# Scores of A's second head by VectorE as well, and the three units of a set in turn

## The chip, the cores and the metric

The kernel runs on one core of a Trainium2 chip. A core has TensorE (PE, matmuls; PEld are its weight loads), VectorE (DVE), ScalarE (ACT), GpSimd (POOL) and SyncE (SP, which here issues the loads); data comes from HBM into SBUF by DMA. The metric is the device time of one execution in microseconds: 1005.88 us, the median of three runs (1005.79 to 1005.91).

## The reference

One token is decoded by two attention blocks over the same input x (448 wide), and a gate mixes their outputs. Block A has 16 heads with a K and a V of their own, block B has 16 query heads on 8 K/V heads. Both caches hold 8192 keys of 256 floats.

```python
    def _A_ref(x, k_cache, v_cache, wq, wo):
        B, Sq, D = x.shape
        H, Dh = 16, 256
        q = (lambda x, *d: x.transpose(*d))((x @ wq).reshape(B, Sq, H, Dh), 0, 2, 1, 3)
        scores = jnp.einsum("bhqd,bhkd->bhqk", q, k_cache) * (Dh ** -0.5)
        p = _softmax(scores, axis=-1)
        o = jnp.einsum("bhqk,bhkd->bhqd", p, v_cache)
        return (lambda x, *d: x.transpose(*d))(o, 0, 2, 1, 3).reshape(B, Sq, H * Dh) @ wo
...
    x = A_x
    g = _sigmoid((x * gate_w).sum(-1, keepdims=True))
    a = _A_ref(x, A_k_cache, A_v_cache, A_wq, A_wo)
    b = _B_ref(x, B_k_cache, B_v_cache, B_wq, B_wo)
    return g * a + (1 - g) * b
```

`_B_ref` does the same with each K and V used for two query heads. All of it is float32. K and V of both blocks are 24 heads x 2 x 8.4 MB, 403 MB, and each byte is used once.

## The kernel before, in words

**Tiles and sets.** The heads are worked off in 8 sets. A set has three units: unit 2 is one K/V head of B with its two queries, units 0 and 1 are two heads of A. A unit's 8192 keys are cut into NT = 4 tiles of 16 rows on each of 128 partitions: a K tile and a V tile have 128 x 4096 floats, 2.1 MB each. TILES (line 35) is the order of all 96 tiles: set by set, in a set unit 2, then 0, then 1, and in a unit its four tiles.

**The stream.** The host lays everything that is read, K, V, wq and wo, into one array in the order of `plan()`. There the K tile with index i is followed by the V tile with index i - LEAD (LEAD = 3), so a V tile comes three tiles behind its K tile. The pieces are cut into loads of FULL = 15872 floats a partition (7936 KB), which go into a ring of SLOTS = 3 slots. SyncE issues a load when all work on the slot's former content is done, and the work on a load waits for the whole of it. The last loads are small: the last half load of V and K, the last V tile in pieces of 8, 4 and 4 rows, and the wo of the last set.

**Scores in two ways.** B's unit 2 and A's unit 1 are scored on TensorE (`scores`): the host has turned their K so that the head's dimension lies on partitions; 8 matmuls write the scores of a tile into PSUM (ps_sc), VectorE takes the minimum (mn), ScalarE the exponential (px), VectorE transposes it into pr. A's unit 0 is scored on VectorE (`scores_by_row`, the units in BY_ROW, line 32): K lies by rows, VectorE multiplies the tile in its slot with the head's query, which `spread` has copied to all partitions (qa), and sums each row (sr); then follow the minimum in three short operations, the exponential on ScalarE (pxr) and the spread into pr.

**The rest of a unit.** `attend` multiplies pr with the V tile on TensorE and adds up in PSUM (ps_o, three buffers, one for each unit under way). After a unit's last K tile, `gather`, `combine` and `column` bring the sums of its 128 partitions together (gs, mnr, ew, es, z, rz, wr, then sel); after its last V tile, `take` moves ps_o into ob by ScalarE and VectorE, and `project_o` makes from ob and sel the column ocs, which wo is multiplied with (`emit_set`, at the end `emit` and `emit_half`, into ps_y).

**What sets the order.** No scheduler: `build` walks through the loads, and `piece` writes the work of each piece in that order on all engines. `combine`, `column` and `project_o` are put off by one or two K tiles (`wait`, `tick`; among the last V tiles each V tile ticks). Each engine runs its instructions in the order written, and `Recorder` adds the semaphores.

Of the kernel before, what the change touches and what calls it, by code (L numbers as in the profile page):

```python
# [3 lines left out]
F32 = mybir.dt.float32  # L4
# [5 lines left out]
P = 128  # L10
D = 448
DH = 256
# [4 lines left out]
NG = 4  # L17
YN = D // NG

NS = 8  # L20
ROWS = 16
NT = NCOL // ROWS
FULL = 15872
LEAD = 3
BLK = 32
NB = ROWS
# [2 lines left out]
SLOTS = 3  # L29
WQ = (4 * KF + 2) * DH  # L30
UNITS = [2, 0, 1]
BY_ROW = {(s, 0) for s in range(NS)}
LAST_CUT = [8, 4, 4]
HEAD_AT = {2: 0, 0: 2, 1: 3}
TILES = [((s, r), t) for s in range(NS) for r in UNITS for t in range(NT)]


DEAL = {0: 8, 1: 7, 2: 8, 4: 8, 7: 8, 8: 8, 15: 8}
# [16 lines left out]
def plan():  # L55

    size = {"xg": XG, "k": ROWS * DH, "v": ROWS * DH, "wq": WQ, "wo": 8 * D}
    per = len(UNITS) * NT
    n = len(TILES)
    items = []  # L60
# [197 lines left out]
def build(nc, stream, dealt, out):  # L258
# [4 lines left out]
    small = Pool(nc, "small", 2)  # L263
# [6 lines left out]
    def heads(u):  # L270
        return 2 if u[1] == 2 else 1
# [6 lines left out]
    for M in (2, 1):  # L278
        r = R[M]
# [7 lines left out]
        CAP[M] = const.tile([P, NT], F32, name=f"cap{M}")  # L287
        nc.vector.tensor_scalar(CAP[M], mask, 3.0e38, OFF, op0=OP.mult, op1=OP.add)

    even = small.tile([P, NB * BLK], F32, name="px")[:, :P].rearrange("p (k n) -> p k n", k=2)  # L290
    nc.gpsimd.iota(even, pattern=[[1, 2], [2, P // 2]], base=0, channel_multiplier=-1,
                   allow_small_or_imprecise_dtypes=True)
    nc.vector.tensor_scalar(even, even, 0.0, None, op0=OP.is_equal)
    half = const.tile([P, 2], F32, name="half")
    nc.vector.tensor_reduce(half, even, axis=AX.X, op=OP.add)

    head2 = small.tile([P, NB * BLK], F32, name="px")[:, :P].rearrange("p (m n k) -> p m n k", m=2, k=2)
    nc.gpsimd.iota(head2, pattern=[[2, 2], [4, P // 4], [1, 2]], base=0, channel_multiplier=-1,
                   allow_small_or_imprecise_dtypes=True)
    nc.vector.tensor_scalar(head2, head2, 0.0, None, op0=OP.is_equal)  # L300
# [10 lines left out]

    in4 = const.tile([P, 2, NG], F32, name="in4")
    nc.vector.tensor_copy(in4[:, 0, :], rows4)
    block = small.tile([P, NB * BLK], F32, name="px")[:, :P].rearrange("p (g n) -> p g n", g=NG)
    nc.gpsimd.iota(block, pattern=[[BLK, NG], [1, BLK]], base=0, channel_multiplier=-1,
                   allow_small_or_imprecise_dtypes=True)
    nc.vector.tensor_scalar(block, block, 0.0, None, op0=OP.is_equal)
# [8 lines left out]
    for par in range(2):  # L326
        for r in (r for r in range(3) if (par, r) not in BY_ROW or (par + 2, r) not in BY_ROW):
            QB[par, r] = const.tile([P, 2, 64], F32, name=f"qb{par}{r}")
# [13 lines left out]
    def clear(t, n):  # L342
        nc.tensor.matmul(t[:, :n], zero, zero[:, None, :n // 4].to_broadcast([P, 4, n // 4]), start=True, stop=False, skip_group_check=True)
# [24 lines left out]
    ST, PR, O, GS, WR, SEL, OB, OC = ({} for _ in range(8))  # L368

    QR, SC, QA = {}, {}, {}  # L370

    def project(s, c0, w):

        if s not in QR:
            QR[s] = ps_s.tile([2 * BLK, 2 * DH], F32, name="sm")
        q = QR[s]
        if s == DS and c0 == KF:
            for j in range(DN):
                k = DN - 1 - j
                n = BLK if j == 0 else 1  # L380
                nc.tensor.matmul(q[:n, :], dx[:, k:k + n], dq[:, k, :], start=(j == 0), stop=False, skip_group_check=True)
        for j in range(w.shape[1]):
            a, c = divmod(c0 + j, KF)
            for a in (a,) if a < 2 else (0, 1):
                c = c if c0 + j < 2 * KF else KF
                nc.tensor.matmul(q[BLK * a:BLK * (a + 1), :], xz[:, c if c < KF else KF + a, :], w[:, j, :],
                                 start=(c == 0), stop=(c == KF), skip_group_check=True)
        if c0 + w.shape[1] == 2 * KF + 1:
            QR[s] = small.tile([P, NB * BLK], F32, name="px")[:2 * BLK, :2 * DH]
            nc.scalar.activation(QR[s], q, AF.Copy)  # L390

    def spread(s):

        qt = ps_s.tile([P, 2, 2, 2], F32, name="sm")
        qr = QR.pop(s)
        for h in range(2):
            for e in range(2):
                at = h * DH + e * P
                nc.tensor.matmul(qt[:, h, e, :], qr[:, at:at + P], rows4[:2 * BLK, :2], start=True, stop=True)
        for r, a, h, M in ((2, 0, 0, 2), (0, 1, 0, 1), (1, 1, 1, 1)):  # L400
            if (s, r) in BY_ROW:
                qa = ps_s.tile([P, DH], F32, name="sm")
                nc.tensor.matmul(qa, rows4[:2 * BLK, 1:2].to_broadcast([2 * BLK, P]), qr[:, h * DH:(h + 1) * DH], start=True, stop=True)
                QA[s, r] = small.tile([P, DH], F32, name="qa", bufs=1)
                nc.scalar.activation(QA[s, r], qa, AF.Copy, scale=-scale)
                continue
            nc.vector.tensor_scalar(QB[s % 2, r][:, :, BLK:BLK + M], qt[:, h:h + M, :, a].rearrange("p h e -> p e h"),
                                    -scale, None, op0=OP.mult)

    def scores(u, t, j0, kt):  # L410
        M = heads(u)
        if t == 0 and j0 == 0:
            ST[u] = small.tile([P, 2, NT], F32, name="st", bufs=4)
        if j0 == 0:
            SC[u, t] = ps_sc.tile([P, NB * BLK], F32, name="sc")
        sc = SC[u, t]
        qb = QB[u[0] % 2, u[1]]
        for j in range(kt.shape[1]):
            e, g = divmod(j0 + j, NG)
            at = BLK - R[M] * g - t * M  # L420
            nc.tensor.matmul(sc[32 * g:32 * (g + 1), :], qb[:, e, at:at + 32], kt[:, j, :],
                             start=(e == 0), stop=(e == 1), skip_group_check=True)
        if j0 + kt.shape[1] < 2 * NG:
            return
        st = ST[u]
        mn = small.tile([P, 1], F32, name="mn")
        nc.vector.tensor_reduce(mn, sc, axis=AX.X, op=OP.min)
        nc.vector.tensor_tensor(st[:, 0, t:t + 1], mn, CAP[M][:, t:t + 1], op=OP.min)
        px = small.tile([P, NB * BLK], F32, name="px")
        nc.scalar.activation(px, sc, AF.Exp, bias=st[:, 0, t:t + 1], scale=-1.0, accum_out=st[:, 1, t:t + 1])  # L430
        pr = small.tile([P, NB * BLK], F32, name="pr", bufs=LEAD + 1)

        nc.vector.transpose(pr.rearrange("p (q r k) -> p q k r", r=BLK, k=2),
                            px.rearrange("p (q k c) -> p q k c", c=BLK, k=2))
        PR[u, t] = pr.rearrange("p (q c) -> p q c", c=2 * BLK)
# [41 lines left out]
    def take(u):  # L477

        o = O.pop(u)
        ob1 = small.tile([P, NB * BLK], F32, name="px")[:, :DH]  # L480
        OB[u] = small.tile([P, DH], F32, name="ob")
        nc.scalar.activation(ob1, o[:, DH:], AF.Copy, scale=half[:, 1:2])
        nc.vector.scalar_tensor_tensor(OB[u], o[:, :DH], half[:, 0:1], ob1, op0=OP.mult, op1=OP.add)

    def gather(u):
# [3 lines left out]
        st = ST[u][:, :, None, :].to_broadcast([P, 2, NG, NT])  # L489
        if u in BY_ROW:  # L490
            nc.vector.tensor_tensor(GS[u][:, :, :, :, 0], st, in4[:, :, :, None].to_broadcast([P, 2, NG, NT]), op=OP.mult)
# [31 lines left out]
    def column(u):  # L523
        M = heads(u)
        cl = ps_s.tile([P, 1], F32, name="sm")
        nc.tensor.matmul(cl, WR.pop(u).rearrange("p c x m k -> p (c x m k)"), ones[:1, :], start=True, stop=True)
        SEL[u] = small.tile([P, 2], F32, name="sel")
        if M == 2:
            nc.vector.tensor_scalar(SEL[u], which, cl, None, op0=OP.mult)
        else:  # L530
            nc.scalar.activation(SEL[u][:, :1], cl, AF.Copy)
# [16 lines left out]

    def fold():

        yf = small.tile([P, NB * BLK], F32, name="px")
        nc.scalar.activation(yf[:, :D], YY[0], AF.Copy)
        YY[0] = ps_y.tile([P, D], F32, name="Y")
        clear(YY[0], YN)
        for g in range(NG):
            nc.tensor.matmul(YY[0][32 * g:32 * g + 1, :YN], any4, yf[:, g * YN:(g + 1) * YN], start=False, stop=False,
                             skip_group_check=True)
# [34 lines left out]
    def wait(n, f, *args):  # L592
        todo.append([n, f, args])

    def tick():
        for t in todo:
            t[0] -= 1
        for t in [t for t in todo if t[0] <= 0]:
            todo.remove(t)
            t[1](*t[2])  # L600

    def piece(kind, i, at, view):
        n = view.shape[-1] // ATOM[kind]
        j0 = at // ATOM[kind]
        if kind == "xg":
            inputs(view)
            GW[0] = view[:, KF + 1:DX]
        elif kind == "wq":
            project(i, j0, view.rearrange("p (c n) -> p c n", c=n))
            if j0 + n < 2 * KF + 1:  # L610
                pass
# [5 lines left out]
        elif kind == "k":  # L617
            u, t = TILES[i]
            if u in BY_ROW:
                scores_by_row(u, t, 2 * j0, view.rearrange("p (j d) -> p j d", d=DH))  # L620
# [9 lines left out]
        elif kind == "v":  # L630
            u, t = TILES[i]
            n = view.shape[-1] // DH
            attend(u, t, at // DH, n, view.rearrange("p (j d) -> p j d", d=DH))
            if at // DH + n == ROWS:
                if t == NT - 1:
                    take(u)
                    if u != TILES[-1][0]:
                        wait(1, project_o, u)
                if i >= len(TILES) - LEAD:
                    tick()  # L640
# [14 lines left out]
    for fill in LOADS:  # L655
        buf = ring.tile([P, FULL], F32, name="slot")
        c = 0
        for load in fill:
            n = sum(x[3] for x in load)
# [84 lines left out]
```

## Time and profile before

| what | before |
| --- | --- |
| median of three runs | 1005.88 us |
| the profiled execution's own time | 1005.68 us |
| its span, first to last instruction | 1004.0 us |
| mean granted TensorE clock | 0.765 |
| read from HBM | 433.07 MB |

The page cuts the span into 40 slices; a digit is a slice's busy share in tenths. These are the rows of TensorE, VectorE, the clock and the loads.

```profile
PE   1665754665653674656645565764665647645567
DVE  3287222962249521486115851248521585215851
PEclk9776687677776886787777867776887877877888
DMA  9999999999999999999999999999999999999998
```

VectorE's row goes up and down eight times, once a set: it is high while unit 0 is scored and low while TensorE scores the other two. The row of the DMA is the same throughout.

Most instructions are recorded under one source line, 198, where the kernel's helper issues them; the groups are told apart by the tiles that they write and read. In a row of a group stand the instruction, what it writes and reads, the shape, the count, then the busy time, the mean of one in ns, and the idle time ahead of it with what ended it. In a row of the timeline stand the start and the duration in us, and in square brackets an idle time ahead of it.

### The profile page before, as it was taken

The numbers are of one execution on the slowest core, as the hardware profiler recorded it, in microseconds if no ns is written. First come the engines' busy times: TensorE is split into PE (matmuls) and PEld (weight loads), VectorE is DVE, ScalarE is ACT, GpSimd is POOL, SyncE is SP. The second block draws the span as 40 slices with busy tenths as digits, with TensorE's granted clock in tenths as the row PEclk, the third lists the DMA queues.
The fourth block names the chain that finished last, engine by engine and source line by source line (L and its number), as shares of the span: only waits on it lengthen the run. The fifth ranks groups of instructions, "written<-read, shape, count | busy, mean of one in ns | idle before, by whom it ended". The sixth has DMA issues, their size and how long they took to land.

```text
span 1004.0 us, 7427 instructions
## 1 busy us (share of the span) xinstructions
PE 593.3 (59%) x3162; PEld 172.6 (17%) x3162; DVE 461.2 (46%) x645; ACT 94.2 (9%) x308; POOL 6.1 (1%) x12
## 2 busy tenths in 40 slices
PE   1665754665653674656645565764665647645567
PEld 0111211121111221112111121111211112111112
DVE  3287222962249521486115851248521585215851
ACT  0100110001100110001100010100110000110011
POOL 2000000000000000000000000000000000000000
PEclk9776687677776886787777867776887877877888
DMA  9999999999999999999999999999999999999998
GB/s 395 442 440 435 423 433 444 433 423 438 443 426 425 441 441 430 423 443 439 426 433 436 438 428 440 430 429 437 436 436 427 431 443 433 426 433 443 435 413 364
DMA packets 9544, 432.49 MB, mean 431 GB/s; under 512 B 1137, under 2 KB 1521, under 8 KB 2161
## 3 DMA queue, kind: packets, MB, share of 16 engines
q1 hardware_dynamic: 9364, 431.24, 99.3%
q0 software_dynamic: 144, 0.79, 0.2%
q8 instruction: 24, 0.39, 0.1%
q14 instruction: 8, 0.07, 0.0%
q10 hardware_dynamic: 4, 0.00, 0.0%
HBM read 433.07 MB, written 0.00 MB: 431 GB/s over the span
## 4 chain that ended last, share of the span: by engine, by line
DMA 71%; PE 15%; DVE 13%; ACT 1%; issue 1%; SPq 0%; DVEq 0%
DMA slot<-in_stream_dram 71%; PE ps_o L198 6%; PE ps_sc L198 6%; DVE sr L198 5%; DVE slot L198 5%; PE ps_s L198 2%; DVE pr L198 1%; ACT px L198 1%; DVE mn L198 1%; ACT ew L198 0%; DVE st L198 0%; DVE wr L198 0%; ACT pxr L198 0%; PE ps_y L198 0%; DVE mt L198 0%
## 5 line engine op out<-in xcount | busy, mean ns | idle before, releaser
L198 PE MATMUL ps_o<-slot,pr 128*32 128x512 f32 (+1 forms) x1536 | 350.7, 762 | 217.4 <-DMA slot<-in_stream_dram 217.3
L198 PE MATMUL ps_sc<-slot,qb 128*32 128x512 f32 x1024 | 201.7, 751 | 98.5 <-DMA slot<-in_stream_dram 98.4
L198 DVE TENSOR_REDUCE mn<-ps_sc 128x1 f32<-128x512 f32 x64 | 44.1, 690 | 327.5 <-PE ps_sc L198 301.9
L198 DVE TENSOR_TENSOR slot<-slot,qa 128x4096 f32<-128x4096 f32 (+7 forms) x40 | 142.6, 3564 | 36.4 <-DMA slot<-in_stream_dram 36.4
L198 PEld LDWEIGHTS ps_o<-slot,pr 128*32 128x32 f32 (+1 forms) x1536 | 80.4, 143 | 399.7 <-DMA slot<-in_stream_dram 245.4
L198 DVE TENSOR_REDUCE sr<-slot 128x16 f32<-128x4096 f32 (+7 forms) x40 | 142.7, 3566 | 1.4
L198 PEld LDWEIGHTS ps_sc<-slot,qb 128*32 128x32 f32 x1024 | 46.9, 134 | 220.5 <-issue 115.8
L198 ACT ACTIVATE px<-ps_sc,st 128x512 f32<-128x512 f32 x64 | 44.0, 687 | 401.9 <-DVE st L198 401.9
L198 DVE STREAM_TRANSPOSE pr<-px 128x512 f32<-128x512 f32 x64 | 45.7, 714 | 54.1 <-ACT px L198 54.1
L198 PE MATMUL ps_s<-slot,xz 128*32 128x512 f32 (+1 forms) x130 | 42.4, 652 | 28.3 <-DVE xz L198 22.1
L198 ACT ACTIVATE pxr<-sr,st 128x16 f32<-128x16 f32 x32 | 9.8, 307 | 365.1 <-DVE st L198 365.1
L198 PE MATMUL ps_s<-sel,ob 128*128 128x1 f32 (+1 forms) x96 | 18.1, 292 | 34.6 <-DVE ob L198 34.6
L198 DVE SCALAR_TENSOR_TENSOR ob<-ps_o,half,px 128x256 f32<-128x256 f32 x24 | 11.3, 472 | 58.5 <-ACT px L198 58.5
L198 PEld LDWEIGHTS ps_s<-sel,ob 128*128 128x128 f32 x96 | 16.0, 235 | 58.9 <-DVE ob L198 47.8
L198 DVE TENSOR_TENSOR pr<-pxr,cols 128x256 f32<-128x256 f32 x32 | 13.6, 426 | 16.9 <-ACT pxr L198 15.5
L198 PE MATMUL ps_y<-slot,ocs 128*1 128x448 f32 (+1 forms) x176 | 18.2, 500 | 3.8 <-DMA slot<-in_stream_dram 3.6
L198 PEld LDWEIGHTS ps_s<-slot,xz 128*32 128x32 f32 (+1 forms) x130 | 10.4, 122 | 54.4 <-issue 25.2
L198 ACT ACTIVATE px<-ps_o,half 128x256 f32<-128x256 f32 x24 | 11.3, 470 | 56.9 <-PE ps_o L198 56.7
L198 PE MATMUL ps_s<-ones,wr 1*128 1x1 f32 x48 | 10.0, 276 | 10.9 <-DVE wr L198 10.9
L198 PE MATMUL ps_s<-px,rows 64*128 64x256 f32 x16 | 7.0, 523 | 13.8 <-DVE es L198 13.8
L198 PEld LDWEIGHTS ps_s<-ones,wr 1*128 1x128 f32 x48 | 8.0, 207 | 34.6 <-DVE wr L198 17.0
L198 ACT ACTIVATION_READ_ACCUMULATOR px<-ps_sc,st 128x1 f32 x64 | 12.3, 193 | 0.0
(68 smaller groups left out, 152.3 us busy)
## 6 DMA issues: line engine op xcount, KB each, us to landing
slot<-in_stream_dram SPq DMA_DIRECT2D x48, 7936.0 KB, 41.2
slot<-in_stream_dram SPq DMA_DIRECT2D x1, 7904.0 KB, 48.5
slot<-in_stream_dram SPq DMA_DIRECT2D x1, 7712.0 KB, 43.8
slot<-in_stream_dram SPq DMA_DIRECT2D x1, 7688.0 KB, 21.0
slot<-in_stream_dram SPq DMA_DIRECT2D x1, 5120.0 KB, 42.3
slot<-in_stream_dram SPq DMA_DIRECT2D x2, 2048.0 KB, 32.7
slot<-in_stream_dram SPq DMA_DIRECT2D x1, 2816.0 KB, 35.8
slot<-in_stream_dram SPq DMA_DIRECT2D x2, 1024.0 KB, 31.2
```

What stands on the lines that cost most here:

```text
L198: i = getattr(e, what)(*args, **kw)
```

## The change

Unit 1 joins BY_ROW, so both A heads of each set are scored by VectorE from rows of K, and its K is laid out by rows in the stream. In TILES the loops over units and tiles change places, so a set's units alternate: tile 0 of unit 2, 0, 1, then tile 1 of the three, and so on. The buffers follow: px has one instead of two, qa four instead of one, sel four instead of two.

```diff
-BY_ROW = {(s, 0) for s in range(NS)}
+BY_ROW = {(s, r) for s in range(NS) for r in (0, 1)}
...
-TILES = [((s, r), t) for s in range(NS) for r in UNITS for t in range(NT)]
+TILES = [((s, r), t) for s in range(NS) for t in range(NT) for r in UNITS]
...
             if (s, r) in BY_ROW:
                 qa = ps_s.tile([P, DH], F32, name="sm")
                 nc.tensor.matmul(qa, rows4[:2 * BLK, 1:2].to_broadcast([2 * BLK, P]), qr[:, h * DH:(h + 1) * DH], start=True, stop=True)
-                QA[s, r] = small.tile([P, DH], F32, name="qa", bufs=1)
+                QA[s, r] = small.tile([P, DH], F32, name="qa", bufs=4)
...
-        px = small.tile([P, NB * BLK], F32, name="px")
+        px = small.tile([P, NB * BLK], F32, name="px", bufs=1)
...
-        SEL[u] = small.tile([P, 2], F32, name="sel")
+        SEL[u] = small.tile([P, 2], F32, name="sel", bufs=4)
...
-        return [t for s in range(NS) for r in UNITS
-                for t in (b[s] if r == 2 else by_row[2 * s + r] if by_row is not None and (s, r) in BY_ROW else a[2 * s + r])]
+        pick = lambda s, r: b[s] if r == 2 else by_row[2 * s + r] if by_row is not None and (s, r) in BY_ROW else a[2 * s + r]
+        return [pick(*u)[t] for u, t in TILES]
```

The other places that take a px tile get `bufs=1` in the same way.

How the instructions move is seen in the order in which they stand on each engine. At the end of the program VectorE had these rows before, from the minimum of the last set's next to last K tile (unit 1) to the end; the units' tiles share one name.

```order
L198 TENSOR_REDUCE mn<-ps_sc 128x1
L198 TENSOR_TENSOR st<-mn,cap_0 128x1
L198 STREAM_TRANSPOSE pr<-px 128x8x2x32
L198 SCALAR_TENSOR_TENSOR ob<-ps_o,half,px 128x256
L198 TENSOR_REDUCE mn<-ps_sc 128x1
L198 TENSOR_TENSOR st<-mn,cap_0 128x1
L198 STREAM_TRANSPOSE pr<-px 128x8x2x32
L198 TENSOR_TENSOR gs_1<-st,pos_0 128x32
L198 TENSOR_REDUCE mnr<-ps_s 1x1
```

The SCALAR_TENSOR_TENSOR is the `take` of unit 0, and the last two rows begin the sums of unit 1. In the changed kernel the last K tile of the program, again unit 1's, stands on VectorE like this, from the end of unit 2's sums on:

```order
L198 TENSOR_SCALAR wr_0<-ew,rz,gate 1x32x2 x2
L198 TENSOR_TENSOR gs_0<-st,in_0 128x32
L198 TENSOR_TENSOR slot<-slot,qa 128x4096
L198 TENSOR_REDUCE sr<-slot 128x16
L198 TENSOR_REDUCE mn<-sr 128x1
L198 STREAM_TRANSPOSE mt<-mn 128x32
L198 TENSOR_REDUCE st<-mt 128x1
L198 TENSOR_TENSOR pr<-pxr,cols 128x256
L198 TENSOR_SCALAR sel<-which,ps_s 128x2
L198 TENSOR_REDUCE mnr<-ps_s 1x1
```

The multiply and the sum over 4096 elements have taken the place of the minimum from PSUM, and the sums of unit 2 and unit 0 now stand directly ahead of and behind that tile, since the three units end within three tiles of each other.

TensorE's last rows before were these: the attends of unit 1's last V tiles with its sums between them, then wo.

```order
L198 MATMUL ps_s<-sel,ob 128x1 x2
L198 MATMUL ps_o<-slot,pr 32x512 x16
L198 MATMUL ps_s<-gs_1,ones 1x32
L198 MATMUL ps_o<-slot,pr 32x512 x8
L198 MATMUL ps_s<-ones,wr_0 128x1
L198 MATMUL ps_o<-slot,pr 32x512 x8
L198 MATMUL ps_y<-slot,ocs 1x112 x8
L198 MATMUL ps_s<-sel,ob 128x1 x2
L198 MATMUL ps_y<-slot,ocs 1x112 x24
```

Now they are these, from the last attend of unit 2 (64x512) on:

```order
L198 MATMUL ps_o<-slot,pr 64x512 x8
L198 MATMUL ps_s<-ones,wr_0 128x1
L198 MATMUL ps_s<-gs_1,ones 1x32
L198 MATMUL ps_s<-sel,ob 128x2 x2
L198 MATMUL ps_o<-slot,pr 32x512 x8
L198 MATMUL ps_s<-ones,wr_0 128x1
L198 MATMUL ps_s<-sel,ob 128x1 x2
L198 MATMUL ps_o<-slot,pr 32x512 x8
L198 MATMUL ps_y<-slot,ocs 1x112 x8
L198 MATMUL ps_s<-sel,ob 128x1 x2
L198 MATMUL ps_y<-slot,ocs 1x112 x24
```

Ahead of unit 0's last attend (the first 32x512) stand unit 0's column (ones, wr), unit 1's sums (gs, ones) and unit 2's projection (sel, ob 128x2); ahead of unit 1's stand unit 1's column and unit 0's projection. Before, one sum and one column stood between the last attends, and a projection ahead of them.

More of the change, by code (lines that the diff above doesn't have):

```diff
@@ L288, in build @@
         nc.vector.tensor_scalar(CAP[M], mask, 3.0e38, OFF, op0=OP.mult, op1=OP.add)
-    even = small.tile([P, NB * BLK], F32, name="px")[:, :P].rearrange("p (k n) -> p k n", k=2)
+    even = small.tile([P, NB * BLK], F32, name="px", bufs=1)[:, :P].rearrange("p (k n) -> p k n", k=2)
     nc.gpsimd.iota(even, pattern=[[1, 2], [2, P // 2]], base=0, channel_multiplier=-1,
@@ L295, in build @@
     nc.vector.tensor_reduce(half, even, axis=AX.X, op=OP.add)
-    head2 = small.tile([P, NB * BLK], F32, name="px")[:, :P].rearrange("p (m n k) -> p m n k", m=2, k=2)
+    head2 = small.tile([P, NB * BLK], F32, name="px", bufs=1)[:, :P].rearrange("p (m n k) -> p m n k", m=2, k=2)
     nc.gpsimd.iota(head2, pattern=[[2, 2], [4, P // 4], [1, 2]], base=0, channel_multiplier=-1,
@@ L313, in build @@
     nc.vector.tensor_copy(in4[:, 0, :], rows4)
-    block = small.tile([P, NB * BLK], F32, name="px")[:, :P].rearrange("p (g n) -> p g n", g=NG)
+    block = small.tile([P, NB * BLK], F32, name="px", bufs=1)[:, :P].rearrange("p (g n) -> p g n", g=NG)
     nc.gpsimd.iota(block, pattern=[[BLK, NG], [1, BLK]], base=0, channel_multiplier=-1,
@@ L388, in project @@
         if c0 + w.shape[1] == 2 * KF + 1:
-            QR[s] = small.tile([P, NB * BLK], F32, name="px")[:2 * BLK, :2 * DH]
+            QR[s] = small.tile([P, NB * BLK], F32, name="px", bufs=1)[:2 * BLK, :2 * DH]
             nc.scalar.activation(QR[s], q, AF.Copy)
@@ L479, in take @@
         o = O.pop(u)
-        ob1 = small.tile([P, NB * BLK], F32, name="px")[:, :DH]
+        ob1 = small.tile([P, NB * BLK], F32, name="px", bufs=1)[:, :DH]
         OB[u] = small.tile([P, DH], F32, name="ob")
@@ L549, in fold @@
     def fold():
-        yf = small.tile([P, NB * BLK], F32, name="px")
+        yf = small.tile([P, NB * BLK], F32, name="px", bufs=1)
         nc.scalar.activation(yf[:, :D], YY[0], AF.Copy)
```

## The prediction

> **What bounds the kernel now.** I read the page's totals first, then the DMA queue, then stretches of one load each.
>
> ```profile
> PE 593.3 (59%) x3162; PEld 172.6 (17%) x3162; DVE 461.2 (46%) x645; ACT 94.2 (9%) x308; POOL 6.1 (1%) x12
> ...
> q1 hardware_dynamic: 9364, 431.24, 99.3%
> ...
> slot<-in_stream_dram SPq DMA_DIRECT2D x48, 7936.0 KB, 41.2
> ```
>
> No engine is near full, and the queue of loads is busy for 99.3% of the span. A full load is 7936 KB. The median load is issued 41.2 us before it lands, so another load is still in front of it: the ring is refilled in time.
>
> The windows below are one load each in the middle of the kernel, and the long middle as a whole (busy time of each engine, then granted clock, DMA share and GB/s).
>
> ```profile
> 437.70:456.40 18.70, 9.06 (x32) 2.65 (x32) 16.95 (x15) 1.16 (x5) 0.00 (x0) 0.77 1.00 435
> 512.60:531.30 18.70, 9.59 (x64) 2.45 (x64) 1.56 (x3) 0.84 (x3) 0.00 (x0) 0.77 1.00 435
> 63.40:913.30 849.90, 512.35 (x2674) 148.88 (x2676) 385.29 (x520) 79.35 (x262) 0.00 (x0) 0.75 1.00 433
> ```
>
> The first has VectorE busy for 16.95 of 18.70 us, the second for 1.56, and both move 435 GB/s. So the transfers bound the kernel, at a rate that does not depend on which engine reads the slots. At 433 GB/s a full load (8.13 MB) takes 18.8 us and one K or V tile (2.10 MB) 4.84 us. A change of engine work can move the time in two places only: where a slot comes free too late for the next load, and behind the last bytes.
>
> **The change, middle of the kernel.** The plan of loads depends on indices alone, so loads, sizes and their order stay, and only which head stands in a tile changes. 32 K tiles move from TensorE to VectorE.
>
> ```profile
> L198 PE MATMUL ps_sc<-slot,qb 128*32 128x512 f32 x1024 | 201.7, 751 | 98.5 <-DMA slot<-in_stream_dram 98.4
> L198 DVE TENSOR_REDUCE sr<-slot 128x16 f32<-128x4096 f32 x24 | 106.1, 4420 | 0.8
> L198 DVE TENSOR_TENSOR slot<-slot,qa 128x4096 f32<-128x4096 f32 x24 | 106.0, 4416 | 20.2 <-DMA slot<-in_stream_dram 20.2
> ...
> 942.56 4.43 DVE L198 TENSOR_TENSOR slot<-slot,qa 128x4096 f32<-128x4096 f32 x1 [3.17 <-DMA slot<-in_stream_dram]
> 952.65 0.43 DVE L198 TENSOR_TENSOR pr<-pxr,cols 128x256 f32<-128x256 f32 x1 [0.54 <-ACT pxr L198]
> 952.99 0.48 DVE L198 SCALAR_TENSOR_TENSOR ob<-ps_o,half,px 128x256 f32<-128x256 f32 x1
> ...
> 910.98 0.69 DVE L198 TENSOR_REDUCE mn<-ps_sc 128x1 f32<-128x512 f32 x1 [1.09 <-PE ps_sc L198]
> 913.52 3.88 DVE L198 TENSOR_TENSOR slot<-slot,qa 128x3584 f32<-128x3584 f32 x1
> ```
>
> TensorE loses half of the 1024 score matmuls, about 101 us, which is worth nothing: it waited for the transfers there. A tile by row holds VectorE from the start of its multiply to the next operation, 942.56 to 952.99 = **10.43 us**: 4.42 + 4.42 and 1.6 for the minimum, ScalarE's exponential and the spread into pr. A B tile holds it 910.98 to 913.52 = **2.54 us**, its wait for ScalarE included. A round of three pairs is now two tiles by row and one of B: 2 x 10.43 + 2.54 = 23.4 us of VectorE against six tiles of transfer, 29.1 us. VectorE has 5.7 us a round for the small work, so the mean holds. Busy time alone grows by 9.9 (10.43 less the 0.54 of waiting) for each of the 32 tiles and falls by the 1.4 that a minimum (0.69) and a transpose (0.71) took: 461 + 32 x 8.5, about 730 us.
>
> The tightest place should be the first load, where the work starts from nothing.
>
> ```profile
> 34.58 0.71 DVE L198 STREAM_TRANSPOSE pr<-px 128x512 f32<-128x512 f32 x1 [0.84 <-ACT px L198]
> 43.67 5.33 PE L198 MATMUL ps_sc<-slot,qb 128*32 128x512 f32 x18 [7.15 <-DMA slot<-in_stream_dram]
> 63.46 1.98 PE L198 MATMUL ps_o<-slot,pr 128*64 128x512 f32 x4 [7.81 <-DMA slot<-in_stream_dram]
> ```
>
> The first B tile ends at 35.29. Behind it now come one tile by row (10.43) and 14/16 of another (twice 3.9), so slot 0 is free at 53.5, where the second load has landed (43.67) and the third lands at 63.46. The fourth is issued some 10 us before the queue runs dry. The next slot, landed at 43.67, holds the rest of that tile (1.4 + 1.6), a B tile and a tile by row, so it is done by 69.5 against a deadline near 82. Hence **0 us** in the middle; a gap there would cost one for one. The wider buffers (qa, sel) add no operation beyond 8 copies into qa on ScalarE (94.2 us busy of 1004); one px buffer less orders ScalarE behind VectorE's transpose, and B tiles now stand a round apart, which covers it.
>
> **The change, end of the kernel.** Here the cover is gone. Before, the last four K tiles were TensorE's; now they are A's head 1, B, head 0, head 1, 33.8 us of VectorE in one line behind the load that lands at 961.3.
>
> ```profile
> 926.85 0.17 DVE L198 TENSOR_REDUCE mnr<-ps_s 1x2 f32<-1x32 f32 x1
> 928.82 4.41 DVE L198 TENSOR_TENSOR slot<-slot,qa 128x4096 f32<-128x4096 f32 x1
> ...
> 961.31 1.07 PE L198 MATMUL ps_o<-slot,pr 128*32 128x512 f32 x2 [3.69 <-DMA slot<-in_stream_dram]
> 967.82 0.12 DVE L198 TENSOR_REDUCE mnr<-ps_s 1x1 f32<-1x16 f32 x1
> 969.11 0.67 DVE L198 TENSOR_REDUCE mn<-ps_sc 128x1 f32<-128x512 f32 x1
> 969.24 0.38 PE L198 MATMUL ps_s<-ones,wr 1*128 1x1 f32 x2 [0.40 <-DVE wr L198]
> 980.11 3.64 PE L198 MATMUL ps_o<-slot,pr 128*32 128x512 f32 x16 [6.92 <-DMA slot<-in_stream_dram]
> 985.84 0.63 PE L198 MATMUL ps_s<-sel,ob 128*128 128x1 f32 x4
> 992.29 1.92 PE L198 MATMUL ps_o<-slot,pr 128*32 128x512 f32 x16 [2.21 <-DMA slot<-in_stream_dram]
> 997.20 1.05 PE L198 MATMUL ps_o<-slot,pr 128*32 128x512 f32 x4 [0.20 <-DMA slot<-in_stream_dram]
> 999.35 0.63 PE L198 MATMUL ps_s<-sel,ob 128*128 128x1 f32 x4 [0.44 <-DVE ob L198]
> 999.91 2.16 PE L198 MATMUL ps_y<-slot,ocs 128*1 128x112 f32 x48
> 1002.42 0.63 SPq L198 DMA_DIRECT2D out_dram<-ys  x1
> ```
>
> The loads still land at 961.3, 980.1, 992.3 and so on to the last quarter of V at 997.2. VectorE: the tile by row from 961.3 to 971.7; B, 2.54, to 974.3; head 0's last tile to 984.7; combine of B (926.85 to 928.82 = 1.97) and a gather (0.2) to 986.9; **head 1's last tile, landed at 980.1, only from 986.9 to 997.3**. Then sel (0.2), combine of head 0 (967.82 to 969.11 = 1.29) and a gather: 999.0; then ob of B (0.5): 999.5.
>
> On TensorE the columns of head 0 wait for that combine (to 999.3), then come the sums of head 1 (0.3), B's projection (0.63, to 1000.2), and only then V of head 0, though it landed at 992.3, and V of head 1. An attend of 16 rows is 1.92 us at full clock (row at 992.29) and 3.64 at half (row at 980.11). B's own V, which stands ahead of these columns, should be done by about 993, so TensorE has idled some 6 us by then, and I take 3.64 for the first, to 1003.9, and 1.92 for the second. From an attend's end to the projection, through ScalarE and VectorE, went 997.20 + 1.05 to 999.35 = 1.10 us. So: projection of head 0 at 1005.0 to 1005.6, V of head 1 to 1007.5, its projection at 1008.6. From that point the program before took 999.35 to 1004.0 = 4.65 us; some 0.4 of this was waiting for the last pieces of wo, now long there: 4.2 us. The span ends at 1012.8 in place of 1004.0: **+8.8 us**. Against the profiled execution's own 1005.68 us (its median stands 0.2 higher) that is 1005.68 + 0 + 8.8 = **1014.5 us**, 0.9% slower.
>
> The clock of TensorE decides the ends of that term. These windows show it around the idle time before 980.11 (PEclk is third from the end).
>
> ```profile
> 976.00:978.00 2.00, 0.00 (x0) 0.00 (x0) 0.00 (x0) 0.00 (x0) 0.00 (x0) 0.92 1.11 479
> 978.00:980.00 2.00, 0.00 (x0) 0.00 (x0) 0.00 (x0) 0.00 (x0) 0.00 (x0) 0.50 0.69 295
> 984.00:985.00 1.00, 1.00 (x12) 0.31 (x8) 0.48 (x1) 0.29 (x1) 0.00 (x0) 0.75 0.92 393
> ```
>
> The clock fell to half during the idle stretch and came back about 4.4 us after work resumed. If it is full all through, both attends cost 1.92: 1012.8. If it stays at half to the end, the second attend costs 1.7 more and the projections and wo matmuls about 1 more: 1017.2.
>
> By the Trainium skill, "TensorE: Matmul & The Clock Gate", Part 1 on the HAM clock gate, the array runs at half rate by default, is released after some 3.4 us of sustained activity and throttled again after an idle window of that length. The rows above agree in kind. Applied to the broken-up work after 999, the rule would keep the half rate longer than I do, and the sum would go towards 1017.2.
>
> **The rivals.**
> 1. **Half clock to the end, 1017.2 us.** For: work in pieces with waits of 1 us between them. Against: the row at 992.29 ran at full rate after a wait of 2.21 us. And its opposite, full clock throughout: 1012.8.
> 2. **The end is hidden, 1005.7 us, not slower.** VectorE would have to begin head 1's last tile when it lands, at 980.1: then it is done at 990.5, before the last V. It decides on whether the work from 961.3 (10.43 + 2.54 + 10.43 + 2.2 = 25.6 us) fits into the 18.8 us between the two landings; a tile by row would have to cost 7.0 us or less. Against it stand 24 multiplies and 24 reductions at 4.42 us each. A stream that runs faster with less TensorE reading would also come out here or below, but the two windows at 435 GB/s speak against it.
> 3. **VectorE becomes the bound, about 1056 us.** It does from 13.3 us a tile by row ((29.1 - 2.54) / 2), or if waits between VectorE and TensorE in their fixed orders eat the 5.7 us of each round. Two us over in each of 32 rounds is 64 us, less the ring's lead of 22 us (41.2 - 18.8): 1014.5 + 42. For it: TensorE's columns wait for VectorE with V tiles behind them, at every set. Against: 16.95 us busy of 18.70 already went by without a gap in the loads.
>
> **How the numbers follow.** Forecast, with the clock as taken: 0.50; full clock 0.18, half clock 0.17; hidden 0.06; faster stream 0.02; VectorE the bound 0.07. The three cases of the end hold 0.85 between 1012.8 and 1017.2; with some 1.3 us for overlaps in the chain of small steps below, and 0.8 above, the range is 1011.5 to 1018. About 0.2% (2 us) is what a measurement of this kernel can tell from no change: faster 0.02, within 0.06, slower 0.92.
>
> **What would show it.** Right: the queue of loads still near 433 GB/s in the middle with a median issue to landing of 37 to 41 us, VectorE at 720 to 740 us busy, the last reduction of 4096 ending near 996, the last attend between 1005 and 1009, and in the chain of waits VectorE and TensorE, not a load, over the last 40 us. Wrong: loads with issue to landing near 19 us (the ring starves), or a last attend that still waits for a load (hidden).

## The result and the profile after

| what | before | after |
| --- | --- | --- |
| median of five runs each | 1005.79 us (1005.62 to 1005.91) | 1016.90 us (1014.82 to 1018.46) |
| ratio, 95% interval | | 1.0105 (1.0093 to 1.0116) |
| the profiled execution's own time, its span | 1005.68, 1004.0 us | 1015.03, 1013.5 us |

The changed kernel is 1.05% slower. Its profiled execution, one of the quicker of its runs, came out 0.5 us above the forecast of 1014.5; the median lies 2.4 us above, in the range, next to the 1017.2 that the prediction gave for the half clock. First the page of the changed kernel: busy time of the engines, the queue of loads, the full loads, and the line of the chain that ended last.

```profile
PE 535.3 (53%) x2666; PEld 160.2 (16%) x2666; DVE 724.5 (71%) x747; ACT 83.7 (8%) x316; POOL 6.2 (1%) x12
...
q1 hardware_dynamic: 9364, 431.24, 98.4%
...
DMA 49%; DVE 37%; PE 9%; ACT 3%; issue 1%; DVEq 0%; SPq 0%
...
slot<-in_stream_dram SPq DMA_DIRECT2D x48, 7936.0 KB, 38.1
```

VectorE went from 461.2 to 724.5 us busy. The same bytes went through the same queue, whose share fell only because the span is longer. A full load is issued 38.1 us before it lands (41.2 before), so the ring still has one whole load in front of it. The windows of the stretches that the prediction looked at say the same (columns as there: PE, PEld, DVE, ACT, POOL, then clock, DMA share, GB/s).

```profile
437.70:456.40 18.70, 8.91 (x48) 2.24 (x48) 10.44 (x12) 1.18 (x4) 0.00 (x0) 0.77 1.00 432
63.40:913.30 849.90, 458.75 (x2228) 137.06 (x2228) 620.36 (x615) 69.04 (x266) 0.00 (x0) 0.73 1.00 433
```

Over 850 us VectorE has 235 us more to do than before (620.36 against 385.29), and the rate is 433 GB/s in both. The middle costs nothing. The end is seen in the timeline of VectorE and TensorE (start, duration, instruction, idle time ahead).

```profile
962.31 4.43 DVE L198 TENSOR_TENSOR slot<-slot,qa 128x4096 f32<-128x4096 f32 x1 [1.70 <-DMA slot<-in_stream_dram]
975.27 4.42 DVE L198 TENSOR_TENSOR slot<-slot,qa 128x4096 f32<-128x4096 f32 x1
...
981.04 3.32 PE L198 MATMUL ps_o<-slot,pr 128*32 128x512 f32 x16 [5.37 <-DMA slot<-in_stream_dram]
...
987.78 4.41 DVE L198 TENSOR_TENSOR slot<-slot,qa 128x4096 f32<-128x4096 f32 x1
997.85 0.43 DVE L198 TENSOR_TENSOR pr<-pxr,cols 128x256 f32<-128x256 f32 x1 [0.54 <-ACT pxr L198]
...
999.77 0.38 PE L198 MATMUL ps_s<-ones,wr 1*128 1x1 f32 x2 [3.10 <-DVE wr L198]
1000.50 0.60 PE L198 MATMUL ps_s<-sel,ob 128*128 128x2 f32 x4 [0.20 <-DVE mnr L198]
1001.03 3.57 PE L198 MATMUL ps_o<-slot,pr 128*32 128x512 f32 x16
1005.72 0.63 PE L198 MATMUL ps_s<-sel,ob 128*128 128x1 f32 x4 [0.82 <-DVE ob L198]
1006.28 1.92 PE L198 MATMUL ps_o<-slot,pr 128*32 128x512 f32 x16
1009.33 0.63 PE L198 MATMUL ps_s<-sel,ob 128*128 128x1 f32 x4 [0.73 <-DVE ob L198]
1009.89 1.33 PE L198 MATMUL ps_y<-slot,ocs 128*1 128x112 f32 x48
```

Three multiplies over 4096 elements follow each other from 962.31. The last one, on a tile that landed at 981.0, starts at 987.78. TensorE's column of head 0 then waits for VectorE's wr, and the two last attends stand behind it, one of them at half rate (3.57 us) and one at full (1.92). Behind the row at 981.04 none waits for a load, as the last rows of before did. The clock in that stretch:

```profile
998.00:1000.00 2.00, 0.23 (x2) 0.23 (x2) 1.56 (x9) 0.62 (x2) 0.00 (x0) 1.00 0.97 384
1002.00:1004.00 2.00, 2.00 (x16) 0.28 (x8) 0.00 (x0) 0.00 (x0) 0.00 (x0) 0.50 0.01 3
1005.00:1006.00 1.00, 0.28 (x3) 0.28 (x3) 0.48 (x1) 0.21 (x2) 0.00 (x0) 1.00 0.00 0
```

It was 1.00 while TensorE stood idle, was 0.50 while the first of the attends ran, and was back for the second.

### The profile page after: what moved, and what is told of

Same layout as the page of the kernel before. It is cut to its first block, busy times and chain, and to the rows that moved or that the text cites. A ratio compares the mean times of both kernels' runs of the same rounds, so it can differ in the third digit from the quotient of the medians.

```text
span 1013.5 us, 6580 instructions
## 1 busy us (share of the span) xinstructions
PE 535.3 (53%) x2666; PEld 160.2 (16%) x2666; DVE 724.5 (71%) x747; ACT 83.7 (8%) x316; POOL 6.2 (1%) x12
## 4 chain that ended last, share of the span: by engine, by line
DMA 49%; DVE 37%; PE 9%; ACT 3%; issue 1%; DVEq 0%; SPq 0%
DMA slot<-in_stream_dram 49%; DVE sr L198 16%; DVE slot L198 15%; PE ps_o L198 5%; PE ps_s L198 2%; DVE pr L198 2%; PE ps_sc L198 2%; ACT px L198 1%; DVE mn L198 1%; ACT pxr L198 1%; DVE st L198 1%; DVE ob L198 1%; DVE mt L198 1%; DVE wr L198 0%; ACT ew L198 0%
## 5 line engine op out<-in xcount | busy, mean ns | idle before, releaser
L198 DVE TENSOR_TENSOR slot<-slot,qa 128x4096 f32<-128x4096 f32 (+7 forms) x80 | 284.6, 3557 | 48.3 <-DMA slot<-in_stream_dram 48.3
L198 DVE TENSOR_REDUCE sr<-slot 128x16 f32<-128x4096 f32 (+7 forms) x80 | 285.3, 3566 | 2.7
L198 PE MATMUL ps_sc<-slot,qb 128*32 128x512 f32 x512 | 93.4, 727 | 35.6 <-DMA slot<-in_stream_dram 35.6
L198 DVE TENSOR_REDUCE mn<-ps_sc 128x1 f32<-128x512 f32 x32 | 21.9, 685 | 89.3 <-PE ps_sc L198 89.2
L198 ACT ACTIVATE pxr<-sr,st 128x16 f32<-128x16 f32 x64 | 19.7, 307 | 675.4 <-DVE st L198 675.4
L198 DVE TENSOR_TENSOR pr<-pxr,cols 128x256 f32<-128x256 f32 x64 | 27.2, 425 | 34.8 <-ACT pxr L198 34.2
L198 DVE STREAM_TRANSPOSE pr<-px 128x512 f32<-128x512 f32 x32 | 22.9, 714 | 27.0 <-ACT px L198 27.0
L198 PEld LDWEIGHTS ps_sc<-slot,qb 128*32 128x32 f32 x512 | 22.3, 138 | 101.6 <-issue 57.6
L198 ACT ACTIVATE px<-ps_sc,st 128x512 f32<-128x512 f32 x32 | 22.0, 687 | 122.5 <-DVE st L198 122.5
L198 DVE STREAM_TRANSPOSE mt<-mn 128x32 f32<-128x32 f32 x64 | 13.5, 212 | 2.2
## 6 DMA issues: line engine op xcount, KB each, us to landing
slot<-in_stream_dram SPq DMA_DIRECT2D x48, 7936.0 KB, 38.1
```

What stands on the lines that cost most here:

```text
L198: i = getattr(e, what)(*args, **kw)
```

## The experiments

All times are medians; each ratio is against the kernel before on the same chip.

**1. The order alone.** Head 0 alone is scored by row, in the alternating order.

```diff
-BY_ROW = {(s, r) for s in range(NS) for r in (0, 1)}
+BY_ROW = {(s, 0) for s in range(NS)}
...
-                QA[s, r] = small.tile([P, DH], F32, name="qa", bufs=4)
+                QA[s, r] = small.tile([P, DH], F32, name="qa", bufs=2)
```

> Alternating order kept, but only head 0 of each set by row, as before (head 1's K tiles go back to TensorE). Theory (the whole loss is VectorE's line of work behind the load of 961.3): the last K tile is TensorE's again, VectorE has one tile by row left (from 968 to about 979), so the last V is the end again: 1005.7 us, at most 1008. Rival (the alternating order itself costs, by projections and columns that now stand between the last attends): 1009 or more.

Measured: 1006.09 us, ratio 0.9999 (0.9990 to 1.0009). In this form the exponentials of head 1 take the one px buffer that holds the next set's queries, so the scores from the second set on come from other queries; the instructions and their sizes are the same. It was run once more with wq two tiles later, which keeps the queries apart:

```diff
-        if i % per == 7 and i // per + 1 < NS:
+        if i % per == 9 and i // per + 1 < NS:
```

> The first experiment (alternating order, head 0 alone by row) with the next set's wq two tiles later, so that no exponential of A's second head takes the px buffer before the queries are spread. Theory: as there, 1005.7 to 1006.5 us.

Measured: 1006.14 us, ratio 1.0001 (0.9992 to 1.0011). The alternating order by itself costs nothing that the times can tell.

**2. The rows alone**, in the old order of units.

```diff
-TILES = [((s, r), t) for s in range(NS) for t in range(NT) for r in UNITS]
+TILES = [((s, r), t) for s in range(NS) for r in UNITS for t in range(NT)]
```

> Both heads by row, but in the old order of units (head 1's four K tiles are the last four). Theory: four tiles by row stand in VectorE's line from 961.3, behind what is left of head 0's, 41.7 us and more: the last one ends near 1006 to 1007, one attend and the rest of the end follow: 1018 to 1021 us, above the changed kernel. The middle still costs nothing (8 tiles by row in a row are 83.4 us of VectorE against 77.4 us of transfer, inside the ring's lead). Rival (the time follows from the amount of work on VectorE, not from where the last tiles stand): the same 1015 to 1018 as the changed kernel. Rival (the ring starves in the long stretches): over 1025.

Measured: 1020.41 us, ratio 1.0144 (1.0128 to 1.0159). In its timeline the last tile by row starts 10 us later than in the changed kernel, and TensorE waits for it:

```profile
997.36 4.42 DVE L198 TENSOR_TENSOR slot<-slot,qa 128x4096 f32<-128x4096 f32 x1
...
1007.95 0.19 PE L198 MATMUL ps_s<-gs,ones 128*1 128x32 f32 x1 [4.50 <-DVE gs L198]
...
1011.79 1.92 PE L198 MATMUL ps_o<-slot,pr 128*32 128x512 f32 x16
1014.83 0.63 PE L198 MATMUL ps_s<-sel,ob 128*128 128x1 f32 x4 [0.73 <-DVE ob L198]
```

So the rows make the loss, and the alternating order takes some 3.5 to 4 us of it back: here the last four tiles on VectorE, from 964.40 on, are all by row, where the changed kernel has three of them and B's from 962.31 on. That this is the reason is read from the two timelines.

**3. The changed kernel with the last set's head 1 on TensorE.** Of the 64 K tiles of A that are scored by row, four go back. (To make room, ys and the masks take other buffers; those lines are left out below.)

```diff
-BY_ROW = {(s, r) for s in range(NS) for r in (0, 1)}
+BY_ROW = {(s, r) for s in range(NS) for r in (0, 1)} - {(NS - 1, 1)}
...
-        for r in (r for r in range(3) if (par, r) not in BY_ROW or (par + 2, r) not in BY_ROW):
+        for r in (r for r in range(3) if any((s, r) not in BY_ROW for s in range(par, NS, 2))):
```

> The changed kernel, with the scores of head 1 of the last set alone given back to TensorE; sets 0 to 6 have both heads by row (ys takes a px buffer and the masks an mt buffer, to make room). Theory (all of the cost is in the end, none in the middle): 1005.7 us, at most 1007.5, and last loads landing near 1001.7 after the start of the span. Rival (56 of 64 tiles by row slow the stream or starve the ring a little): 1007.5 to 1016, in proportion to the tiles moved.

Measured: 1006.06 us, ratio 1.0001 (0.9992 to 1.0010), VectorE 691.8 us busy. The end of its timeline waits for loads again:

```profile
997.26 1.92 PE L198 MATMUL ps_o<-slot,pr 128*32 128x512 f32 x16
1000.29 0.63 PE L198 MATMUL ps_s<-sel,ob 128*128 128x1 f32 x4 [0.73 <-DVE ob L198]
...
1002.52 0.36 PE L198 MATMUL ps_y<-slot,ocs 128*1 128x112 f32 x4 [0.20 <-DMA slot<-in_stream_dram]
```

Seven sets with both heads by row cost nothing that the times can tell (spans 1004.6 to 1005.0, against 1004.0 to 1004.4 before); the loss hangs on the four K tiles of the last set's head 1. Which of the four matter was not tried one by one. (The expectation counts 56 tiles, those of the first seven sets; head 0's four of the last set make 60.)

**4. The changed kernel once more**, for its spread.

> The changed kernel once more, for the spread of its runs (1014.8 to 1018.5, where before has 1005.6 to 1005.9). If the spread is the clock of TensorE in the last 15 us, its profile shows the same landings as the first and another PEclk and other durations of the last two attends; if it is the stream, the last load lands at another time and the rest behind it is the same 11 us.

Measured: 1016.55 us (1015.02 to 1018.93), ratio 1.0114 (1.0098 to 1.0129). Its profiled execution has the first one's end again, an attend of 3.61 and one of 1.92 us, and the same span to 0.2 us. The spans of all nine executions of the changed kernel lie in groups: 1013.5, 1013.5, 1013.5, 1013.7; 1015.6, 1015.7, 1015.8; 1017.0, 1017.5. The steps are 1.5 to 2 us, where an attend at half rate costs 1.7 us more. Only executions of the lowest group were profiled, so what the others did is not seen in a trace. The mean granted clock of each execution is on record: 0.741 or 0.742 in the lowest group, 0.731 to 0.739 in the others. That agrees with the clock as the cause and does not prove it, since it is a mean over the whole span. The next experiment turns the question round.

**5. The clock.** Twelve small matmuls on zeros, which nothing reads, fill TensorE's idle time ahead of head 0's column.

```diff
+            if i == len(TILES) - LEAD and at // DH + n == ROWS:
+                warm = ps_sc.tile([P, D], F32, name="sc")
+                for _ in range(12):
+                    nc.tensor.matmul(warm, zero, zero[:, None, :D // 4].to_broadcast([P, 4, D // 4]), start=True, stop=True, skip_group_check=True)
```

> The changed kernel with 12 small matmuls on zeros behind the attend of B's last V tile, into a score buffer that is free by then; nothing reads them. They fill TensorE's idle 3 us ahead of the columns of head 0. Theory (the runs of the changed kernel differ by the clock that the last two attends meet: spans near 1013.5, 1015.7 and 1017.3): the first of the two attends takes 1.92 in place of 3.6 us, most spans are 1011.5 to 1012.5, times near 1013.3. Rival (the spread is the stream's or the matmuls delay the columns): 1015 to 1019 as before.

Measured: 1012.69 us (1012.45 to 1015.29), ratio 1.0077 (1.0060 to 1.0093); spans 1011.2, 1011.3, 1011.4 and one of 1014.0. Its timeline:

```profile
995.70 2.44 PE L198 MATMUL ps_sc<-zero 128*128 128x448 bf16 x12
999.10 0.38 PE L198 MATMUL ps_s<-ones,wr 1*128 1x1 f32 x2 [0.96 <-DVE wr L198]
...
1000.37 1.92 PE L198 MATMUL ps_o<-slot,pr 128*32 128x512 f32 x16
...
1003.97 1.92 PE L198 MATMUL ps_o<-slot,pr 128*32 128x512 f32 x16
```

The column still waits for VectorE's wr, VectorE's line has the same length (it starts 0.7 us sooner), and both attends now run at full rate. So 2.44 us of added work make the kernel quicker. Of the 2.3 us between the two profiled spans the first attend gives 1.65 (3.57 to 1.92) and the sooner start 0.7. The median fell by about 4 us (1016.55 to 1012.69, on two chips); that the clock gives all of this is argued, not seen, and the mean clock doesn't sort these four executions (0.738 in the shortest, 0.739 in the longest).

**6. TensorE's order.** The put-off work of the last V tiles comes one V tile later.

```diff
-                if i >= len(TILES) - LEAD:
+                if i > len(TILES) - LEAD:
```

> The changed kernel with the put-off work of the last three V tiles one V tile later: head 0's column, head 1's sums and B's projection stand behind head 0's last attend in place of ahead of it, and head 1's column behind the last attend. VectorE's line is the same length. Theory (the end is VectorE's line plus TensorE's fixed order, which holds landed V tiles back behind columns that wait for VectorE): head 0's attend runs in TensorE's idle time before 999.8, only one attend (1.9) stands between head 0's column and head 1's projection, span near 1009.2, 1009.5 to 1012.5 us. Rival (VectorE's line alone sets the end, as its last sums end at 1001.7 either way): 1014 or more.

Measured: 1013.27 us (1012.16 to 1013.81), ratio 1.0068 (1.0051 to 1.0085), above the range expected, below the rival's.

```profile
999.27 0.38 PE L198 MATMUL ps_s<-ones,wr 1*128 1x1 f32 x2 [1.43 <-DVE wr L198]
...
1002.36 3.64 PE L198 MATMUL ps_o<-slot,pr 128*32 128x512 f32 x16
...
1007.15 0.63 PE L198 MATMUL ps_s<-sel,ob 128*128 128x1 f32 x4
```

The column waits for wr as ever, but one attend instead of two comes behind it. The expectation took that one at 1.92 us; it ran at half rate, 3.64: the clock was at 0.50 from 1001 to 1006, though TensorE's idle time ahead of the column was 1.43 us alone. With seven matmuls on zeros behind head 0's attend as well:

```diff
+            if i == len(TILES) - LEAD + 1 and at // DH + n == ROWS:
+                warm = ps_sc.tile([P, D], F32, name="sc")
+                for _ in range(7):
+                    nc.tensor.matmul(warm, zero, zero[:, None, :D // 4].to_broadcast([P, 4, D // 4]), start=True, stop=True, skip_group_check=True)
```

> The eighth kernel (attends first) with 7 small matmuls on zeros behind head 0's last attend, ahead of its column. Theory (the two gains are separate: the order holds one attend less back, the clock halves the other): the last attend takes 1.92 in place of 3.64 us, span 1009.3 to 1010, time near 1011. Rival (7 matmuls don't lift the clock, or they delay the column): 1012 to 1014.

Measured: 1012.23 us (1010.47 to 1014.43), ratio 1.0064 (1.0045 to 1.0082). That is in the range of the rival. The last attend took 2.96 us in the profiled execution (span 1010.5), where the clock was 0.95 from 1002 to 1003 and 0.50 from there on; the spans go from 1009.2, about what was expected of all, to 1013.1. The matmuls did not hold the clock up to the end in the execution that was profiled; whether order and clock add up stays open.

**7. Another unit last.** B is the last unit of each round, so its K tile, cheap on VectorE, is the last to land.

```diff
-UNITS = [2, 0, 1]
+UNITS = [0, 1, 2]
...
-        if i % per == 7 and i // per + 1 < NS:
+        if i % per == 6 and i // per + 1 < NS:
...
-            if j0 == 2:
-                project_o((NS - 1, 1))
+            if j0 == 0:
+                project_o((NS - 1, 2))
```

> The changed kernel, all 64 A tiles by row, with B as the last unit of each round in place of the first (units 0, 1, 2; the next set's wq one tile earlier so that its queries are spread before B's next tile uses px). Theory (the cost is the place of the last tiles in VectorE's line, not their number): the tiles by row stand behind the loads of 961.3 and 968, the K tile that lands at 980 is B's and costs VectorE 2.5 us, so all sums are done before the last V at 997: 1005.7 to 1007.5 us. Rival (the amount of work on VectorE sets it): 1014 or more.

Measured: 1017.54 us, ratio 1.0115 (1.0098 to 1.0132). The theory as written there falls. Its timeline:

```profile
968.41 0.69 DVE L198 TENSOR_REDUCE mn<-ps_sc 128x1 f32<-128x512 f32 x1 [3.02 <-PE ps_sc L198]
...
993.13 0.58 PE L198 MATMUL ps_s<-ones,wr 1*128 1x1 f32 x2 [6.00 <-DVE wr L198]
...
993.84 7.95 PE L198 MATMUL ps_o<-slot,pr 128*64 128x512 f32 x32
...
996.48 0.34 DVE L198 TENSOR_SCALAR wr<-ew,rz,gate 1x128 f32<-1x128 f32 x1
...
1003.46 1.92 PE L198 MATMUL ps_o<-slot,pr 128*32 128x512 f32 x16
...
1007.06 3.65 PE L198 MATMUL ps_o<-slot,pr 128*64 128x512 f32 x16
```

VectorE is through with both heads' sums at 996.8, some 5 us sooner than in the changed kernel. But head 0 now ends its tiles one place earlier, and its column stands ahead of the last four attends, B's next to last among them. TensorE waits 6.00 us for it, till 993.13, with four attends behind it (the first two are one row). The clock was 0.50 at the first of them and 1.00 from 1000 on. The last one's 3.65 us are no half rate: B's attends have 64 columns of weights where a head of A has 32, and the clock was full while it ran.

```profile
998.00:1000.00 2.00, 2.00 (x12) 0.52 (x12) 0.00 (x0) 0.00 (x0) 0.00 (x0) 0.80 1.01 400
1007.00:1009.00 2.00, 2.00 (x12) 0.82 (x13) 0.00 (x0) 0.17 (x1) 0.00 (x0) 1.00 0.00 0
```

So with B last the longest of the attends stands last as well. VectorE also began late: two tiles by row share the load ahead, and it stood idle 3.02 us for B's scores. Putting the tile that is cheapest for VectorE last is not enough; here the time went by what TensorE had to hold back until VectorE's line was through.

**8. How much the middle can hide.** A second sum over a half, the whole, or a quarter of each K tile by row in sets 0 to 6, which nothing reads.

```diff
+        if u[0] < NS - 1:
+            nc.vector.tensor_reduce(small.tile([P, BLK], F32, name="mt")[:, :n // 2], kt[:, :n // 2, :], axis=AX.X, op=OP.add)
```

> The changed kernel with a second sum over half of each K tile by row in sets 0 to 6, into a tile that nothing reads: 2.2 us more, 12.65 us a tile. Rule of the prediction (VectorE becomes the bound at 13.3 us a tile): the middle still hides it, 1014 to 1022 us with the end unchanged. Rival (the small work and the waits in fixed order already fill the round): 1030 or more.

> The same with a second sum over the whole tile: 4.4 us more, 14.85 us a tile. By the prediction's rule VectorE is now the bound in sets 0 to 6: a set needs 8 x 14.85 + 4 x 2.54 + some 8 us of small work = 137 us against 125 us of transfer, 12 us a set over seven sets, less the ring's lead of 22: 1075 to 1100 us, with idle time of the loads and VectorE over 90% busy. Rival (waits in fixed order cost more than the small work counted): up to 1160.

> The changed kernel with a second sum over a quarter of each K tile by row (pieces of four rows or more) in sets 0 to 6: 1.1 us more, 11.55 us a tile, about 60 us of VectorE in all. Revised rule (a half and a whole more lost about 17 and 139 us, so some 107 us of spare VectorE time, 1.9 us a tile, are hidden in seven sets): nothing is lost, 1014 to 1019 us. Rival (the loss begins at once, in proportion): 1024 or more.

The last is for pieces of four rows or more; it was expected after the other two had been seen. Measured, one run each: a half 1033.28 us (span 1031.7), the whole 1155.0 us (span 1153.7), a quarter 1015.78 us (span 1014.5). The engines' lines of a half, of the whole, and of a quarter:

```profile
PE 515.5 (50%) x2666; PEld 163.6 (16%) x2666; DVE 841.0 (82%) x818; ACT 83.4 (8%) x316; POOL 6.2 (1%) x12
```

```profile
PE 522.0 (45%) x2666; PEld 165.8 (14%) x2666; DVE 960.3 (83%) x818; ACT 83.0 (7%) x316; POOL 6.2 (1%) x12
```

```profile
PE 533.4 (53%) x2666; PEld 166.3 (16%) x2666; DVE 779.8 (77%) x814; ACT 83.7 (8%) x316; POOL 6.2 (1%) x12
```

Against the changed kernel's profiled execution (724.5 us busy, span 1013.5) VectorE does 116.5, 235.8 and 55.3 us more, and the span grows by 18.2, 140.2 and 1.0. So 98 and 96 us were hidden in the first two, nearly the same amount, and nearly all of the third. Against the expectations, the half and the whole came out with the rivals (1030 or more, up to 1160), not with the prediction's rule (1014 to 1022, 1075 to 1100); the quarter came out as expected. **The spare time is some 97 us over 56 tiles, 1.7 us a tile**: VectorE becomes the bound at about 12.2 us a tile by row. With the whole sum the loads idle in the middle and VectorE still isn't full; the window and VectorE's waits show both:

```profile
300.00:900.00 600.00, 270.09 (x1368) 87.39 (x1367) 511.95 (x420) 42.31 (x164) 0.00 (x0) 0.69 0.88 374
```

```profile
DVE mn L198 <- PE ps_sc L198: 52.2, 9, 7.6
DVE pr L198 <- ACT pxr L198: 33.0, 64, 0.9
DVE ob L198 <- ACT px L198: 30.3, 9, 4.2
```

## Why the prediction was right, and where its sizes were off

**The bound, right.** The transfers run at 433 GB/s in the changed kernel as before, with 235 us more of VectorE's work beside them. They fell off where VectorE had more to do than the loads leave time for: 374 GB/s with the whole second sum of experiment 8.

**The middle at nothing, right.** Experiment 3 has 60 tiles by row at a ratio of 1.0001. The 730 us forecast for VectorE's busy time were 724.5.

**The end, right by its mechanism and nearly to the step.** Forecast and profiled execution, in us: head 1's last tile from 986.9 to 997.3, was 987.8 to 998.3; head 0's column done at 999.3, was 1000.15; its V done at 1003.9, was 1004.6; head 1's V 1007.5, was 1008.2; its projection 1008.6, was 1009.3; end 1012.8, was 1013.5. All of it is shifted by 0.7 to 1.0, and so was the load that starts the line, which landed at 962.3 in place of 961.3. From the projection to the end 4.2 us were taken, and 4.2 it was. One step came out by luck. The half rate of the first attend was taken because B's own V would be done by 993 and TensorE idle for 6 us; B's attend ended at 996.67, the idle time was 3.10 us, the clock was at 1.00 all through it and fell at about 1001. That it fell just ahead of this attend was not among the forecast's reasons.

**The clock, right as a rival and too lightly weighted.** The forecast took one attend at half rate and one at full, which is the profiled execution and four of nine spans. The median lies with the groups above. The half clock had a chance of 0.17 and 1017.2 us; five of nine spans are 2 to 4 us above the lowest. Two of the nine times, 1018.46 and 1018.93, lie above the range, and no case of the sum reaches them. The step that failed is the weight, "Against: the row at 992.29 ran at full rate after a wait of 2.21 us". The length of a wait does not settle the clock: in experiment 6 the half rate came after a wait of 1.43 us with some 10 us of work ahead of it. What does settle it stays open. Experiment 5 shows the clock's share in the lowest group; none of the longer executions was profiled.

The Trainium skill, "TensorE: Matmul & The Clock Gate", Part 1, says that the rate falls after an idle window of about 3.4 us and that this window runs free of the program. The trace bears out the kind, not the figure as an idle time: an idle stretch of 3.10 us, shorter than that window, with 1.2 us of small matmuls behind it, was enough for the half rate.

**VectorE as the bound, right as not happening, its threshold off.** The step "It does from 13.3 us a tile by row" counted the round's 29.1 us as if waits could be filled; waits that eat the round's spare time stood beside it as a condition, and they were the case. Measured: about 12.2. Two of the waits in the view above were not in the sum: nine times, about once a set, VectorE stands for B's scores, up to 7.6 us, 52 us in all, and nine times for ScalarE's half of ob, 30 us in all. The small work was not in the 13.3 either, nor the loads of wq and wo; with some 8 us of the one and 125 us of transfer a set, as the expectation of the whole sum has them, the sum still gives about 13.4, so by that sum the waits are what is left. That TensorE gives B's scores late because its own line stands behind a column is argued from its order; it wasn't tried by itself.

**Hidden, not so, but close by.** The line of 25.6 us against 18.8 between the landings decided as written. With one tile by row less in it, and the last tile on TensorE as well (experiment 3), the end is before's to within a microsecond.

## What to carry to other kernels

When transfers bound a kernel, more work on an idle engine is free in the middle up to a point (here 1.7 us a tile by row beyond the change itself), and up to that point its price is read from the last two or three loads alone: list what stands in each engine's line behind them, in the order written. Look there above all for small operations that wait for another engine ahead of large ones whose data is there already. Leaving the last set's second head to TensorE took away the whole loss here; moving the small operations took away a third of it. And where TensorE works in pieces, work the end out at the half rate as well as the full, and don't count on every execution to come out at the same of the two.

## What the runs showed of the hardware that was not expected

The changed kernel has a spread of its own: its spans lie between 1013.5 and 1017.5 us, in steps of 1.5 to 2 us, where those of the kernel before lie between 1004.0 and 1004.4 in the 21 executions beside them. An end that hangs on short bursts of TensorE does not spread by that alone: experiment 2 ends in such bursts, its first attend at half rate too (3.6 us), and its four spans lie between 1018.8 and 1019.1. Twelve matmuls of 448 columns, 2.44 us of work that nothing reads, took 3.9 us off the changed kernel's median (1016.55 to 1012.69).
